# Two weight matrices converted to float32 during the attention, kept in DRAM, and only split later

## The chip, the cores and the metric

The kernel runs on one core of one Trainium2 chip. A core has four computing engines, each with its own instruction queue that runs in order: TensorE (matmul), VectorE, ScalarE and GpSimd. SyncE (SP) issues the DMAs; they too are issued in the order of its queue, so a DMA that waits for a semaphore holds back those behind it. The metric is the time of one execution in microseconds (us). The kernel before takes 804.85 us, the median of 3 runs (803.93 to 806.13).

## The reference, cut

Causal attention with a bias from cumulative sums, then a product of gated projections, then a second feed-forward block with a softmax-weighted activation and a layer norm:

```python
attn_out = attention(q, k, v, s)              # B=4, H=8, S=576, D=64
x = attn_out.transpose(0, 2, 1, 3).reshape(B * S, H * D)      # 2304 x 512
# first block: w1, w2 512x1024, w3 1024x1024, w_out 1024x512
a = x @ w1;  b = x @ w2
x = (a * b @ w3) @ w_out
# second block: w_in 512x1024, w_out2 1024x512, g_ln 1024
h = x @ w_in
solu = h * softmax(h)
ln = (solu - mean(solu)) / sqrt(var(solu) + 1e-6) * g_ln
return ln @ w_out2
```

The six weight matrices arrive as float64. The kernel takes their bit patterns as pairs of 32-bit words and makes float32 of them on the chip.

## The kernel before, in words

**Precision.** TensorE multiplies in a reduced float32 format. Each operand is therefore held as two words, a high one (a copy rounded to that format, `hi`, mostly on ScalarE) and a low one (the rest, `lo`, a subtraction on VectorE or GpSimd), and each product is three matmuls: high by high, high by low, low by high. Names that end in H and L (or h and l) are such pairs.

**Conversion of a weight.** A `stage` tile holds 128 x 512 float64 values (512 KB) as word pairs. `to_f32` (L365) makes float32 of them in place: one scaling of the high words on GpSimd (L371) or ScalarE (L369), then three integer instructions on VectorE (L375, L376, L379). `split_w` (L384) then writes high and low word. `w_job` queues a load and its conversion; `pump(n)` converts n queued tiles and reloads the stage buffers that come free.

**Stages**, with their place in the traced execution:
- Attention, 0 to about 376 us: 32 heads in steps (L504 to 567), scores, softmax, transposes of the probabilities (`tr`), product with v (`av`). The matmuls of a = x w1 and b = x w2 of finished batches (`ab_unit`, L310) are filled in between. During steps 3 to 16, `PUMP` converts the 16 tiles of w1 and w2. g = a b goes to DRAM (`g_scr`).
- The last batch of `ab_unit`, about 376 to 424 us, beside the conversion of w_out (8 tiles) and of the first w3 tiles (16 in all).
- M = w3 w_out, 424 to 468 us: eight blocks `m_unit(f)` (L585) of 24 matmuls into PSUM, each copied out as MH (ScalarE) and ML (VectorE). After each block `pump(AM[f])` converts three more tiles, first the rest of w3, then the eight of w_in (into IH and IL, L744 to 751).
- Second phase, from 468 us: `x2_unit` (x2 = g M in chunks of 256 tokens, L654), `h_unit` (h = x2 w_in and the chain of the layer norm, L678), `tr2` (L714) transposes the normalised tile `so`, `out_unit` (L728) multiplies by w_out2. The eight tiles of w_out2 are converted, scaled by g_ln on ScalarE (L771) and split into OH and OL by `wo2_conv` (L769) during the first x2 and h units.

The order of instructions on each engine is made by a scheduler at build time from the order of the program's text and modelled durations. It decides where a conversion stands in an engine's queue.

Of the kernel before, what the change touches and what calls it, by code (L numbers as in the profile page):

```python
# [25 lines left out]
def tile_attention_moe(  # L26
# [42 lines left out]
    const = ctx.enter_context(tc.tile_pool(name="const", bufs=1, side="left"))  # L69

    g_scr = [dram.tile([KF, 128, S], F32, name=f"g_scr{n}") for n in range(B)]
    cum_scr = dram.tile([NH, 2, S], F32R, name="cum_scr")
# [23 lines left out]
    def lo(dst, src, hi_, eng=nc.vector):  # L96
        eng.tensor_tensor(out=dst, in0=src, in1=hi_.bitcast(F32), op=ALU.subtract)  # L97
# [266 lines left out]

    def to_f32(raw, eng=nc.gpsimd):  # L365

# [3 lines left out]
        else:  # L370
# [6 lines left out]
            out=low, in0=high, scalar=3, in1=low, op0=ALU.logical_shift_left, op1=ALU.bitwise_or,  # L377
        )
        nc.vector.scalar_tensor_tensor(  # L379
            out=low, in0=high, scalar=0x80000000, in1=low, op0=ALU.bitwise_and, op1=ALU.bitwise_or,  # L380
        )
        return low.bitcast(F32)

# [10 lines left out]
    MAT = ()  # L394
    WO2 = (0, 4, 0, 0, 0, 2, 2)
    XMS = ((0,), (1,), (2,), (3,))
    EX = 0
    AP3, AM = (2, 2, 2, 2, 2, 2, 1, 1), (3, 3, 3, 3, 3, 3, 3, 3)
    mjobs = []
# [36 lines left out]
    def wab_job(f, w):  # L436
        fs = slice((f % 4) * 128, (f % 4) * 128 + 128)
        w_job(
            (w1, w2)[w][f],
            lambda: (wab[f // 4][2 * w][:, :, fs], wab[f // 4][2 * w + 1][:, :, fs]),  # L440
            WENG[f] if not isinstance(WENG[f], tuple) else WENG[f][w],
        )


# [48 lines left out]
    for f in range(KF):  # L493
        for w in range(2):
            wab_job(f, w)
    load_jobs()


# [5 lines left out]
    PD, AVO = 10, 2  # L504
    PUMP = {3: 1, 5: 1, 7: 1, 8: 1, 9: 1, 10: 1, 11: 1, 12: 2, 13: 2, 14: 2, 15: 2, 16: 1}
    fill = []
# [64 lines left out]
    ML = pm.tile([128, KF, DM], F32R, name="ML")  # L571
    stg[:] = pm, 4
    mctx = ExitStack()
    mp = mctx.enter_context(tc.tile_pool(name="mp", bufs=1, side="left"))
    WOH = mp.tile([128, KF, DM], F32R, name="WOH")
    WOL = mp.tile([128, KF, DM], F32R, name="WOL")
# [166 lines left out]
    load_g(1)  # L743
    win = []  # L744
    for i in range(8):
        c, o = divmod(i, 2)
        fs = slice(o * 512, o * 512 + 512)
        w_job(
            w_in[c * 128:c * 128 + 128, o * 1024:o * 1024 + 1024],
            lambda c=c, fs=fs: (IH[:, c, fs], IL[:, c, fs]),  # L750
        )
    for f in range(nm[0], KF):
        m_unit(f)
        pump(AM[f] if f < KF - 1 else len(jobs) + len(loaded))
        if f == 4:
            split_g(0, 0)
        if f == 5:
            split_g(0, 1)
# [3 lines left out]
    OL = p2.tile([128, KF, DM], F32R, name="OL")  # L762
    raws = {}

    def wo2_load(k):
        if k < KF:
            raws[k] = stage(wo2[k * 128:k * 128 + 128])

    def wo2_conv(k):  # L769
        t = to_f32(raws.pop(k), G)  # L770
        nc.scalar.activation(out=t, in_=t, func=AF.Copy, scale=gln[:, k:k + 1])  # L771
        hi(OH[:, k], t)
        lo(OL[:, k], t, OH[:, k], nc.gpsimd)
        wo2_load(k + 4)

    nwo = [0]

    def wo2_pump(c):
        for _ in range(c):
            wo2_conv(nwo[0])  # L780
            nwo[0] += 1

    for k in range(4):
        wo2_load(k)
    wo2_pump(WO2[0])
    for i, ms in enumerate(XMS):
        x2_unit(0, *ms)
        wo2_pump(WO2[1 + i])
    split_g(1, 0)
# [5 lines left out]
    for t in range(NT + 2):  # L795
# [9 lines left out]
        if t < 2:  # L805
            wo2_pump(WO2[5 + t])
        if 0 <= t - 2 < NT:
# [57 lines left out]
```

## Time and profile before

| | us |
|---|---|
| median of 3 runs | 804.85 (803.93 to 806.13) |
| profiled execution | 805.43 |
| its span on the core | 803.6 |
| TensorE busy | 764.2 |
| VectorE busy | 454.8 |
| ScalarE busy | 350.9 |
| GpSimd busy | 264.0 |

The span runs from the first to the last instruction. Busy time is the time in which an engine has at least one instruction under way. Matmuls overlap, so a stream of them counts as fully busy even when one starts every 0.12 us and lasts 0.28; the pauses of TensorE are what the table of waits shows. In the rows further down PE is TensorE, PEld its weight loads, DVE VectorE, ACT ScalarE and POOL GpSimd; L12 is line 12 of the kernel; an operation is written out<-in.

### The profile page before, as it was taken

What the parts mean: (1) busy time and instruction counts of PE and PEld (TensorE: products, weight loads), DVE (VectorE), ACT (ScalarE), POOL (GpSimd) and SP (SyncE); (2) the same over time, 40 slices, a digit from 0 to 9 for tenths busy, and PEclk for the clock granted to TensorE, in tenths of its full rate; (3) what the DMA queues carried; (4) which work ended last, traced back from release to release, by engine and by line L of the source; (5) the groups of instructions that cost most, each with busy time, mean ns of one, the idle gap of its engine ahead of it and who ended that gap; (6) DMA issues with size and microseconds to landing.
All of it is one profiled execution on the core that took longest, in us unless ns stands there. A gap on an engine that the chain in (4) does not pass through costs nothing.

```text
span 803.6 us, 13134 instructions
## 1 busy us (share of the span) xinstructions
PE 764.2 (95%) x4848; PEld 652.4 (81%) x4848; DVE 454.8 (57%) x1057; ACT 350.9 (44%) x847; POOL 264.0 (33%) x339
## 2 busy tenths in 40 slices
PE   4897979999999999999999979899999999999997
PEld 2554878888888889888988868788888888888886
DVE  5687688766444554424995999835344243533231
ACT  3674556676545555322434434624333232432231
POOL 7757385967445534201432445400000000000000
PEclk9898999999999999999999989999999999999999
DMA  6344343543333231013668655122020200000001
GB/s 164 109 149 141 113 137 117 148 104 96 99 104 91 76 91 45 31 46 141 209 199 265 226 174 172 58 66 66 14 66 14 67 25 14 14 14 14 14 28 39
DMA packets 38040, 75.59 MB, mean 94 GB/s; under 512 B 6796, under 2 KB 18060, under 8 KB 37976
## 3 DMA queue, kind: packets, MB, share of 16 engines
q1 hardware_dynamic: 37976, 74.76, 30.3%
q8 instruction: 38, 0.62, 0.3%
q14 instruction: 26, 0.21, 0.1%
HBM read 60.36 MB, written 14.38 MB: 93 GB/s over the span
## 4 chain that ended last, share of the span: by engine, by line
PE 79%; DVE 10%; DMA 5%; issue 3%; POOL 2%; ACT 1%; SPq 0%; DVEq 0%; POOLq 0%; ACTq 0%
PE o L734 13%; PE h L685 11%; PE b L333 10%; PE x L665 10%; PE a L333 10%; PE av L305 7%; PE tr L273 4%; PE m L591 3%; PE sc L183 3%; DVE stage L376 3%; DVE stage L375 3%; DMA stage<-in_w_dram 2%; PE sc L191 2%; PE sc L192 2%; PE tr L723 2%
## 5 line engine op out<-in xcount | busy, mean ns | idle before, releaser
L209 ACT ACTIVATE P<-P,STAT 64x64 f32<-64x64 f32 (+4 forms) x160 | 88.2, 553 | 72.3 <-DVE STAT L205 72.0
L241 POOL TENSOR_SCALAR P<-P,STAT 128x576 f32<-128x576 f32 (+4 forms) x160 | 87.0, 563 | 38.7 <-DVE STAT L237 36.5
L707 POOL TENSOR_TENSOR sv<-sv,mhalf 128x1 f32<-128x1 f32 x18 | 10.0, 555 | 262.1 <-DVE sv L704 262.1
L205 DVE CUSTOM_DVE_ANT_0 P<-sc,wmask 64x64 f32<-64x64 f32 (+4 forms) x160 | 71.6, 482 | 26.8 <-PE sc L192 14.5
L693 DVE TENSOR_REDUCE sv<-h 128x1 f32<-128x1024 f32 x18 | 22.0, 1224 | 114.1 <-PE h L685 114.1
L665 PE MATMUL x<-gh,MH 128*128 128x256 f32 x288 | 83.1, 289 | 3.7 <-ACT MH L92 3.7
L665 PE MATMUL x<-gh,ML 128*128 128x256 f32 x288 | 81.5, 284 | 2.1 <-DVE ML L97 2.1
L665 PE MATMUL x<-gl,MH 128*128 128x256 f32 x288 | 81.7, 284 | 0.0
L97 POOL TENSOR_TENSOR QA<-qk,QB 64x576 fp32r<-64x576 f32 x24 | 37.9, 1581 | 84.2 <-ACT QB L92 75.6
L371 POOL TENSOR_SCALAR stage<-stage 128x512 f32<-128x512 f32 x40 | 33.1, 829 | 95.2 <-PE a L333 37.0
L333 PE MATMUL b<-xT0h,W 128*128 128x288 f32 x256 | 60.7, 308 | 3.3 <-DVE g_sb L353 3.2
L94 DVE COPY PT<-tr 64x128 f32<-64x128 f32 (+5 forms) x112 | 41.1, 383 | 34.5 <-ACT PT L92 11.0
L333 PE MATMUL b<-xT1h,W 128*128 128x288 f32 x256 | 59.3, 303 | 1.3 <-ACT a_sb L345 0.7
L333 PE MATMUL a<-xT0h,W 128*128 128x288 f32 x256 | 59.4, 306 | 0.0
L665 PEld LDWEIGHTS x<-gh,MH 128*128 128x128 f32 x288 | 55.5, 193 | 4.7 <-ACT MH L92 3.9
L305 PE MATMUL av<-PT,vr 64*64 64x64 f32 (+4 forms) x384 | 57.9, 414 | 0.3 <-DVE PT L94 0.3
L333 PE MATMUL a<-xT1h,W 128*128 128x288 f32 x256 | 58.0, 300 | 0.0
L353 DVE TENSOR_TENSOR g_sb<-b,a_sb 128x288 f32<-128x288 f32 x64 | 28.7, 452 | 51.3 <-PE b L333 27.7
L734 PE MATMUL o<-OH,lh 128*128 128x512 f32 x144 | 57.2, 397 | 0.3 <-ACT lh L92 0.3
L685 PE MATMUL h<-IH,x2l 128*128 128x512 f32 x144 | 56.7, 394 | 0.8 <-DVE x2l L97 0.8
L665 PEld LDWEIGHTS x<-gh,ML 128*128 128x128 f32 x288 | 55.4, 193 | 2.4 <-DVE ML L97 2.3
L734 PE MATMUL o<-OH,ll 128*128 128x512 f32 x144 | 57.1, 396 | 0.0
(121 smaller groups left out, 2022.8 us busy)
## 6 DMA issues: line engine op xcount, KB each, us to landing
stage<-in_w_dram SPq DMA_DIRECT2D x32, 512.0 KB
qk<-in_qk_dram SPq DMA_DIRECT2D x48, 288.0 KB
g_scr<-g_sb SPq DMA_DIRECT2D x32, 288.0 KB
stage<-in_wo_dram SPq DMA_DIRECT2D x16, 512.0 KB
graw<-g_scr SPq DMA_DIRECT2D x6, 1024.0 KB
out_dram<-o SPq DMA_DIRECT2D x18, 256.0 KB
vr<-in_vm_dram SPq DMA_DIRECT2D x16, 256.0 KB
stage<-in_w_in_dram SPq DMA_DIRECT2D x8, 512.0 KB
```

The source lines that it names most:

```text
L94: eng.tensor_copy(out=dst, in_=src)
L97: eng.tensor_tensor(out=dst, in0=src, in1=hi_.bitcast(F32), op=ALU.subtract)
L205: nc.vector.tensor_tensor_reduce(out=dst2, in0=ps_in, in1=msk, scale=-SCALE, scalar=BIG, op0=ALU.add, op1=ALU.min, accum_out=st[0:rows, ti ...
L209: nc.scalar.activation(out=dst, in_=dst, func=AF.Exp, bias=st[0:rows, ti:ti + 1], scale=-1.0, accum_out=st[0:rows, 5 + ti:6 + ti],)
L241: nc.gpsimd.tensor_scalar(out=dst, in0=dst, scalar1=r, scalar2=1.0, op0=ALU.mult, op1=ALU.mult)
L273: nc.tensor.transpose(ps[:, c:c + 128], pt[:, QOF[i] + 128 * j:QOF[i] + 128 * j + 128], ident)
L305: nc.tensor.matmul(st["ps"][64 * e:64 * e + 64, 448 + c0:448 + c1], vr[0:rows, j, e], PT[(2 * p + e) % 4][0:rows, o + c0:o + c1], **kw,)
L333: nc.tensor.matmul(ps, w_[:, c, fs], x_[:, c, sl], start=(c == 0 and w_ is WH and x_ is XH), stop=(c == KC - 1 and w_ is WL),)
L371: eng.tensor_scalar(out=high.bitcast(F32), in0=high.bitcast(F32), scalar1=2.0 ** -112, scalar2=1.0, op0=ALU.mult, op1=ALU.mult,)
L665: nc.tensor.matmul(ps[m], w_[:, k, m * 128:m * 128 + 128], g_[:, k], start=(k == 0 and w_ is MH and g_ is GH), stop=(k == KF - 1 and w_ is ...
L685: nc.tensor.matmul(ps[:, hf], x_[:, k, ts_], w_[:, k, hf * 512:hf * 512 + 512], start=(k == 0 and x_ is XH and w_ is IH), stop=(k == KC - ...
L734: nc.tensor.matmul(ps, l_[:, k], w_[:, k], start=(k == 0 and l_ is LH and w_ is OH), stop=(k == KF - 1 and l_ is LL),)
```

## The change

The 16 tiles of w_in and w_out2 are no longer converted while M and the second phase run. During steps 19 to 34 of the attention, one a step, each is loaded, converted to float32 (the scaling on ScalarE), w_out2's tiles also scaled by g_ln, written to a new tile `cst` and stored in DRAM (`wf_scr`, 256 KB a tile). While M runs, the float32 tiles are loaded back into four buffers `wf`; `wf_split` makes the high word on ScalarE and the low word on VectorE, one tile of w_in after each `m_unit`, and the eight of w_out2 in the first two rounds of the second phase's loop. `AM` now converts two tiles after each of the first five blocks of M and none after the others. The stage buffers lie in the pool of M's operands instead of the longer-lived one.

```diff
+    wf_scr = [dram.tile([128, CW], F32, name=f"wf_scr{i}") for i in range(16)]
...
-    def to_f32(raw, eng=nc.gpsimd):
+    def to_f32(raw, eng=nc.gpsimd, dst=None):
...
+        res = low if dst is None else dst.bitcast(U32)
         nc.vector.scalar_tensor_tensor(
-            out=low, in0=high, scalar=0x80000000, in1=low, op0=ALU.bitwise_and, op1=ALU.bitwise_or,
+            out=res, in0=high, scalar=0x80000000, in1=low, op0=ALU.bitwise_and, op1=ALU.bitwise_or,
         )
-        return low.bitcast(F32)
+        return res.bitcast(F32)
...
-    WO2 = (0, 4, 0, 0, 0, 2, 2)
...
-    AP3, AM = (2, 2, 2, 2, 2, 2, 1, 1), (3, 3, 3, 3, 3, 3, 3, 3)
+    AP3, AM = (2, 2, 2, 2, 2, 2, 1, 1), (2, 2, 2, 2, 2, 0, 0, 0)
...
+    def spill_job(i):
+        src = w_in[i // 2 * 128:i // 2 * 128 + 128, i % 2 * 1024:i % 2 * 1024 + 1024] if i < 8 else wo2[(i - 8) * 128:(i - 7) * 128]
+
+        def conv(raw):
+            t = at.tile([128, CW], F32, tag="cst", bufs=2, name="cst")
+            to_f32(raw, None, t)
+            if i >= 8:
+                nc.scalar.activation(out=t, in_=t, func=AF.Copy, scale=gln[:, i - 8:i - 7])
+            nc.sync.dma_start(out=wf_scr[i], in_=t)
+
+        jobs.append((src, conv))
...
+    for i in range(16):
+        spill_job(i)
...
-    PUMP = {3: 1, 5: 1, ..., 15: 2, 16: 1}
+    PUMP = {3: 1, 5: 1, ..., 15: 2, 16: 1, 19: 1, 20: 1, ..., 33: 1, 34: 1}
...
-    stg[:] = pm, 4
...
+    stg[:] = mp, 4
...
-    win = []
-    for i in range(8):
-        ...
-        w_job(w_in[...], lambda c=c, fs=fs: (IH[:, c, fs], IL[:, c, fs]))
+    wf = {}
+
+    def wf_load(i):
+        if i < 16:
+            wf[i] = r2.tile([128, CW], F32, tag="wf", bufs=4, name="wf")
+            nc.sync.dma_start(out=wf[i], in_=wf_scr[i])
+
+    def wf_split(i, eng):
+        t = wf.pop(i)
+        if i < 8:
+            c, fs = i // 2, slice(i % 2 * 512, i % 2 * 512 + 512)
+            h_, l_ = IH[:, c, fs], IL[:, c, fs]
+        else:
+            h_, l_ = OH[:, i - 8], OL[:, i - 8]
+        hi(h_, t)
+        lo(l_, t, h_, eng)
+        wf_load(i + 4)
+
+    for i in range(4):
+        wf_load(i)
     for f in range(nm[0], KF):
         m_unit(f)
-        pump(AM[f] if f < KF - 1 else len(jobs) + len(loaded))
+        pump(AM[f])
+        wf_split(f, V)
...
-    def wo2_conv(k):
-        ...
...
         if t < 2:
-            wo2_pump(WO2[5 + t])
+            for k in range(4):
+                wf_split(8 + 4 * t + k, V)
```

What VectorE has in its queue around the last blocks of M and the first units of x2. Before, from the low word of block 5 on (IL is the low word of w_in, stage any tile under conversion):

```order
L97 TENSOR_TENSOR ML<-m,MH 128x512
L379 SCALAR_TENSOR_TENSOR stage<-stage 128x512
L376 SCALAR_TENSOR_TENSOR stage<-stage 128x512
L375 TENSOR_SCALAR stage<-stage 128x512
L379 SCALAR_TENSOR_TENSOR stage<-stage 128x512
L97 TENSOR_TENSOR IL<-stage,IH 128x512
L376 SCALAR_TENSOR_TENSOR stage<-stage 128x512
L375 TENSOR_SCALAR stage<-stage 128x512
L379 SCALAR_TENSOR_TENSOR stage<-stage 128x512
L97 TENSOR_TENSOR ML<-m,MH 128x512
```

The same place on VectorE in the changed kernel, from the last conversion row of w3 on (OL is the low word of w_out2, wf a float32 tile that was loaded back):

```order
L382 SCALAR_TENSOR_TENSOR stage<-stage 128x512
L99 TENSOR_TENSOR w3l<-stage,w3h 128x512
L99 TENSOR_TENSOR ML<-m,MH 128x512 x2
L99 TENSOR_TENSOR OL<-wf,OH 128x512 x4
L99 TENSOR_TENSOR x2l<-x_5346,x2h 128x256
L99 TENSOR_TENSOR x2l<-x_5373,x2h 128x256
L99 TENSOR_TENSOR OL<-wf,OH 128x512 x3
L99 TENSOR_TENSOR x2l<-x_5400,x2h 128x256
L99 TENSOR_TENSOR OL<-wf,OH 128x512
L99 TENSOR_TENSOR x2l<-x_5427,x2h 128x256
L99 TENSOR_TENSOR gl<-graw,gh 128x512 x4
L709 TENSOR_REDUCE sv<-h 128x1
```

The conversion rows of w_in that stood between the ML rows are gone, and so are those of w_out2 between the x2l rows; in their place stand one subtraction a tile, those of w_out2 behind the last ML.

What SP issues while M runs. Before (graw are loads of g, in_w_dram is w3, the others are w_in and w_out2):

```order
L633 DMA graw<-g_scr_66 128x8x256 x2
L414 DMA stage<-in_w_dram 128x1024 x2
L633 DMA graw<-g_scr_66 128x8x64
L633 DMA graw<-g_scr_67 128x8x192
L414 DMA stage<-in_w_dram 128x1024
L633 DMA graw<-g_scr_67 128x8x256
L414 DMA stage<-in_w_dram 128x1024 x4
L414 DMA stage<-in_w_in_dram 128x1024 x8
L414 DMA stage<-in_wo_dram 128x1024 x5
```

SP at the same place in the changed kernel, up to the last w3 load:

```order
L765 DMA wf<-wf_scr_68 128x512
L416 DMA stage<-in_w_dram 128x1024
L765 DMA wf<-wf_scr_69 128x512
L416 DMA stage<-in_w_dram 128x1024
L649 DMA graw<-g_scr_82 128x8x64
L649 DMA graw<-g_scr_83 128x8x192
L416 DMA stage<-in_w_dram 128x1024
L649 DMA graw<-g_scr_83 128x8x256
L765 DMA wf<-wf_scr_70 128x512
L765 DMA wf<-wf_scr_71 128x512
L416 DMA stage<-in_w_dram 128x1024
L765 DMA wf<-wf_scr_72 128x512
```

The loads of float32 tiles stand between those of w3, eight of them (the first two ahead of this piece, one more behind it) ahead of the last three w3 loads; loads of w_in stood behind all w3 loads.

A conversion in the attention of the changed kernel, as VectorE has it in one head's step (L207 is the softmax's first pass, L96 a copy out of PSUM, L355 the product g):

```order
L377 TENSOR_SCALAR stage<-stage 128x512
L378 SCALAR_TENSOR_TENSOR stage<-stage 128x512
L207 ISA P,STAT_116<-sc,wmask 128x320
L207 ISA STAT_116 128x1
L207 ISA P,STAT_116<-sc,wmask 128x192
L207 ISA STAT_116 128x1
L96 CAST QA<-qk_2466 64x576
L382 SCALAR_TENSOR_TENSOR cst<-stage 128x512
L355 TENSOR_TENSOR g_sb<-b,a_sb 128x288
```

Its three instructions stand between those of the softmax; in the kernel before the same rows stand there without them.

## Rows read from the trace of the kernel before

**Rows 1.** The page: busy us, share, instructions; and the chain by engine

```profile
PE 764.2 (95%) x4848; PEld 652.4 (81%) x4848; DVE 454.8 (57%) x1057; ACT 350.9 (44%) x847; POOL 264.0 (33%) x339
...
PE 79%; DVE 10%; DMA 5%; issue 3%; POOL 2%; ACT 1%; SPq 0%; DVEq 0%; POOLq 0%; ACTq 0%
```

**Rows 2.** Busy by stretch: length, each engine's us (instructions), clock, DMA share, GB/s

```profile
80.00:120.00 40.00, 35.44 (x241) 30.96 (x239) 30.84 (x72) 21.10 (x56) 23.84 (x28) 0.96 0.40 121
120.00:160.00 40.00, 39.96 (x300) 34.24 (x298) 32.49 (x84) 25.05 (x72) 29.81 (x32) 1.00 0.45 134
160.00:360.00 200.00, 200.00 (x1499) 173.23 (x1498) 96.94 (x325) 105.08 (x306) 88.00 (x118) 1.00 0.28 78
424.00:468.00 44.00, 43.70 (x193) 36.22 (x194) 35.11 (x52) 18.81 (x32) 15.66 (x12) 1.00 0.73 237
468.00:525.00 57.00, 46.95 (x298) 43.02 (x297) 50.77 (x80) 29.19 (x52) 26.53 (x24) 0.91 0.41 131
525.00:800.00 275.00, 274.62 (x1577) 239.12 (x1575) 104.57 (x210) 87.02 (x163) 8.77 (x16) 1.00 0.10 32
```

**Rows 3.** TensorE's waits, 468 to 525: us, times, longest

```profile
PE x L665 <- ACT MH L92: 3.7, 1, 3.7
PE tr L723 <- DVE so L708: 3.5, 1, 3.5
PE x L665 <- DVE ML L97: 2.1, 1, 2.1
PE h L685 <- DVE x2l L97: 0.8, 1, 0.8
```

**Rows 4.** Timeline of VectorE and ScalarE: start us, duration us, instruction

```profile
471.78 0.68 DVE L97 TENSOR_TENSOR ML<-m,MH 128x512 fp32r<-128x512 f32 x1
...
476.51 0.59 ACT L92 ACTIVATE MH<-m 128x512 fp32r<-128x512 f32 x1
```

**Rows 5.** Busy by stretch, as rows 2, around two pauses

```profile
477.20:481.10 3.90, 3.90 (x18) 3.90 (x19) 3.39 (x5) 1.43 (x3) 2.56 (x3) 0.50 0.45 139
481.40:487.20 5.80, 5.80 (x52) 5.80 (x52) 5.45 (x10) 2.13 (x4) 2.97 (x4) 1.00 0.76 246
512.40:515.30 2.90, 2.90 (x14) 2.90 (x15) 2.19 (x5) 1.82 (x4) 1.07 (x1) 0.50 0.00 0
```

**Rows 6.** Groups by line, 424 to 525: count, busy us, mean ns, idle before

```profile
L376 DVE SCALAR_TENSOR_TENSOR stage<-stage 128x512 uint32<-128x512 uint32 x23 | 20.2, 877 | 0.8 <-POOL stage L371 0.5
L379 DVE SCALAR_TENSOR_TENSOR stage<-stage 128x512 uint32<-128x512 uint32 x23 | 19.0, 825 | 0.1
L375 DVE TENSOR_SCALAR stage<-stage 128x512 uint32<-128x512 uint32 x23 | 16.0, 695 | 1.3 <-DMA stage<-in_wo_dram 0.8 <-DMA stage<-in_w_in_dram 0.3
L371 POOL TENSOR_SCALAR stage<-stage 128x512 f32<-128x512 f32 x16 | 14.9, 931 | 23.9 <-DMA stage<-in_w_dram 7.7 <-DMA stage<-in_wo_dram 4.7 <-DMA stage<-in_w_in_dram 4.0
L97 POOL TENSOR_TENSOR OL<-stage,OH 128x512 fp32r<-128x512 f32 x8 | 12.7, 1603 | 5.7 <-ACT OH L92 5.7
...
L369 ACT ACTIVATE stage<-stage 128x512 f32<-128x512 f32 x7 | 4.7, 674 | 6.1 <-DMA stage<-in_w_in_dram 6.1
```

**Rows 7.** The chain in order of time: start us, us, matmuls

```profile
534.41 5.49 PE h L685 x24
539.90 2.81 PE x L665 x24
```

**Rows 8.** Timeline of GpSimd and VectorE near the last w3 tiles

```profile
453.28 1.90 POOL L97 TENSOR_TENSOR w3l<-stage,w3h 128x512 fp32r<-128x512 f32 x1 [3.23 <-ACT w3h L92]
...
453.93 1.80 DVE L376 SCALAR_TENSOR_TENSOR stage<-stage 128x512 uint32<-128x512 uint32 x1
461.09 1.15 DVE L97 TENSOR_TENSOR w3l<-stage,w3h 128x512 fp32r<-128x512 f32 x1
```

**Rows 9.** Busy by stretch, as rows 2, while M runs

```profile
428.00:448.00 20.00, 20.00 (x90) 16.54 (x90) 15.64 (x23) 9.57 (x17) 7.68 (x5) 1.00 1.04 340
448.00:468.00 20.00, 20.00 (x90) 16.58 (x89) 19.04 (x29) 8.57 (x14) 7.98 (x7) 1.00 0.50 164
```

More of the change, by code (lines that the diff above doesn't have):

```diff
@@ L504, in tile_attention_moe @@
     PD, AVO = 10, 2
-    PUMP = {3: 1, 5: 1, 7: 1, 8: 1, 9: 1, 10: 1, 11: 1, 12: 2, 13: 2, 14: 2, 15: 2, 16: 1}
+    PUMP = {3: 1, 5: 1, 7: 1, 8: 1, 9: 1, 10: 1, 11: 1, 12: 2, 13: 2, 14: 2, 15: 2, 16: 1, 19: 1, 20: 1, 21: 1, 22: 1, 23: 1, 24: 1, 25: 1, 26: 1, 27: 1, 28: 1, 29: 1, 30: 1, 31: 1, 32: 1, 33: 1, 34: 1}
     fill = []
@@ L743, in tile_attention_moe @@
     load_g(1)
-    win = []
-    for i in range(8):
[L746 to L751, printed above, removed]
+    wf = {}
[15 more added lines that the diff above has]
+        wf_load(i)
     for f in range(nm[0], KF):
         m_unit(f)
-        pump(AM[f] if f < KF - 1 else len(jobs) + len(loaded))
+        pump(AM[f])
+        wf_split(f, V)
         if f == 4:
@@ L762, in tile_attention_moe @@
     OL = p2.tile([128, KF, DM], F32R, name="OL")
[L763 to L767, printed above, removed]
-    def wo2_conv(k):
[L770 to L785, printed above, removed]
     for i, ms in enumerate(XMS):
         x2_unit(0, *ms)
-        wo2_pump(WO2[1 + i])
     split_g(1, 0)
```

## The prediction

> **What bounds the kernel now.** I read the page's sums and chain first, then the busy time by stretch, then what TensorE waited for in the one stretch where it stands still late in the run, and only then the rows of VectorE and ScalarE that it waited for. The page shows TensorE busy for 764.2 us of 803.6 and a chain that is 79% TensorE [rows 1]. The stretches show where the rest lies [rows 2]. From 160 to 360 us (the attention) TensorE is busy for all 200 us, and VectorE for 97 and ScalarE for 105 of them. From 424 to 468 (the product M) it is full too. From 525 to 800 (the second phase) it is full again, with VectorE at 105 of 275. Between them, from 468 to 525, VectorE is busy for 50.8 of 57 us, TensorE has only 46.95, and its granted clock is 0.91. So one stretch of 57 us late in the kernel is set by VectorE and the rest by TensorE. That stretch is the one which the change empties.
>
> What TensorE waits for there are four things [rows 3]: the high word of the last M block (3.7 us), the low word of the M block before it (2.1), the normalised row tile of the second phase (3.5) and a low word of x2 (0.8), 10.1 us in all. None of them needs w_in or w_out2. The rows show why they are late [rows 4]: the low word of M block 6 starts on VectorE at 471.78, and its matmuls had ended by about 462.3 (the 424 to 468 row has 193 matmuls in 43.70 us [rows 2], so 226 ns each, 5.43 us a block of 24, and seven blocks from 424.3); MH of block 7 starts on ScalarE at 476.51, 8.5 us after the end of its matmuls at 468. Both engines work in order, and conversions of w_in, some of them waiting for their DMA, stand ahead.
>
> The pauses also cost clock [rows 5]. After the pause that ends at 477.15 TensorE is granted 0.50 (1.2 GHz) and 18 matmuls take 3.90 us; back at 1.00 (2.4 GHz) 52 of the same take 5.80. That is 217 against 112 ns, so 18 x 0.105 = 1.9 us lost. The pause that ends at 512.37 is followed by 2.90 us at 0.50, of which half, 1.45 us, is lost.
>
> **The change part by part, and the sum.** The profiled execution took 805.43 us for a span of 803.6, 0.6 above the median of 804.85; the sum is made against 805.43.
>
> *Removed in the stretch.* Sixteen conversions (eight of w_in, eight of w_out2) leave 424 to 525. Each has three VectorE instructions of 877, 825 and 695 ns there [rows 6], so 16 x 2.40 = 38.4 us of VectorE. On GpSimd twelve scalings of 931 ns go (all of w_out2, half of w_in) and twelve low-word subtractions of about 1.6 us, 30 us in all. On ScalarE eight g_ln scalings and four word scalings go, some 9 us. *Added there.* The twelve subtractions move to VectorE, at 0.68 us each [rows 4], 8.2 us; the high words stay on ScalarE. VectorE's net is minus 30 us of the 86 it has from 424 to 525 [rows 2]. Then it is no longer what ends last. The order shows the same: ahead of the last two ML rows there now stand only w3 conversions, the four OL rows come behind both, and behind the second-phase row maximum no conversion is left. All four waits of [rows 3] have lost what made them late. With the clock that is 10.1 + 1.9 + 1.45 = 13.4 us. As a check from the other side: the stretch holds 216 matmuls of x2 at 2.81/24 us, 72 of h at 5.49/24 [rows 7] (counted in the order) and 8 transposes that I put at 1 us together, 25.3 + 16.5 + 1.0 = 42.8 of 57 us, so 14.2 are lost. I take 14.0 as all there is to win.
>
> *What is late next.* The M product needs its 16 halves of w3, one each the weights of 12 matmuls. In the kernel before the last low half starts on VectorE at 461.09 and takes 1.15 [rows 8]; TensorE reads it from 468 - 12 x 0.226 = 465.3, so the margin is 3.0 us. The change pushes on it from two sides. SP's order puts eight loads of float32 copies (256 KB each, 2.1 MB) in front of the last w3 loads, on a queue that is saturated from 428 to 448: 340 GB/s at a DMA share of 1.04 [rows 9]. If all 2.1 MB fall ahead of the last w3 half at that rate they take 6.2 us. But the queue then falls to 164 GB/s and half share from 448 to 468 [rows 9], and the order pulls two matmuls of the last block and eighteen of x2 in front of the last w3 halves (2 x 0.226 + 18 x 0.117 = 2.6 us of cover). On the other side VectorE loses the w_in conversions there. GpSimd's remaining w3 subtractions still stretch VectorE: 1.80 us for an L376 beside a GpSimd subtraction of 1.90 us, against 877 mean [rows 6, 8]. From below: no wait (6.2 - 3.0 - 2.6 is about nothing, and VectorE is freer); from above: the whole 6.2 us, plus 1.9 for the clock, 8.1. I walked the after order with these durations and found the halves of block 6 just in time; I take 2.0 us, near the lower end, and keep 0 to 8.1.
>
> *Added in the attention.* Sixteen conversions at one a step, sixteen steps that fill about the 200 us from 160 to 360. Each is a ScalarE scaling (674 ns), three VectorE instructions (2.40 us) [rows 6], for the eight of w_out2 a further ScalarE pass that I put at the same, and on SP a 512 KB load and a 256 KB store. That is 38 us of VectorE on 97 and 16 of ScalarE on 105 [rows 2]: 135 and 121 of 200. SP waits in front of each store until VectorE or ScalarE has written it; behind it stand the q and k loads of two heads ahead, the cum rows and the g stores. A step is some 12 us (200/16) and the loads are two ahead, so a store that is late by a few us stays covered. The bounds come from the two stretches that already do this. From 120 to 160 with four to five conversions in 40 us, GpSimd doing part of them, VectorE is at 32.5 and TensorE still at 39.96: cost nothing. From 80 to 120 TensorE has 35.44 of 40 with VectorE at 30.8 [rows 2]: 4.6 us per 40, which over 200 us is 23. The nearer row is 120 to 160 (the same fill matmuls, full clock, a heavier load than is to come), so I take 0.5. Below nothing is excluded, since TensorE is already full and no wait of it is removed there.
>
> *Elsewhere.* Stage buffers that move from one pool to the other, and the 424 us before M: same order, nothing. The splits of w_out2 wait for no DMA on the chain; out_unit reads them, by the order, behind 240 matmuls of x2 and 72 of h, over 40 us.
>
> Sum: 805.4 - 14.0 + 2.0 + 0.5 = 793.9, so 794.
>
> A page speaks against part of this. The Trainium skill, "DMA: Bandwidth & Descriptors", section "Bandwidth", advises batches of 1 MiB and more and gives 341 GB/s there and 138 at 64 KB; the 256 KB pieces fall between, and by an estimate of mine from these two, 240, the 2.1 MB would cost 8.7 us instead of 6.2. By that the sum would be 796 to 797; that page measured single transfers, and no row here shows a saturated stretch of 256 KB pieces.
>
> **The rivals.** (1) *w3 becomes the wait.* The upper bound above, 8.1 us, falls on the chain: 805.4 - 14.0 + 8.1 + 0.5 = 800.0. For it: the saturated queue and a margin of 3.0 us. Against: the half-empty queue behind it. (2) *The attention stops being covered*, and the kernel ends slower: the conversions sit in VectorE's and ScalarE's order ahead of PSUM evictions, the full TensorE of 160 to 360 turns into that of 80 to 120, 23 us: 805.4 - 14 + 2 + 23 = 816. It decides from 14 - 2 = 12 us, that is 2.4 us of standing in each 40. For it: each conversion holds VectorE for over 2 us at a stretch; against: 120 to 160. (3) *The change does not do what it says*: M's evictions on ScalarE stay in order behind high-word splits that wait for the float32 copies' DMA as they did behind w_in, so that the 3.7 and 2.1 and their 1.9 of clock stay, half of rival 1's 8.1 comes on top, and only the second pause goes: 805.4 - 14 + 7.7 + 4 = 803.1. For it: ScalarE in the after order still has four such splits between M's evictions; against: SP's order has eight of these loads ahead of the last w3 loads, and had those of w_in behind them.
>
> **How the numbers follow.** My forecast (790 to 798) 0.65, rival 1 (798 to 802.4) 0.20, rival 3 0.07, rival 2 0.08. A difference under 0.3%, 2.4 us, can't be told from none here. Forecast and rival 1 are faster, 0.85; rival 3 is the same, 0.07; rival 2 slower, 0.08. The range for 8 in 10 goes from 789.5 (nothing new waits, and a little more comes off than the check shows) to 802 (rival 1 with its clock): it leaves out rivals 2 and 3 and a small tail below.
>
> **What would show it.** Right: from 468 to 525 no wait of TensorE for MH, ML or the normalised tile over 1 us, granted clock 1.00 there, VectorE below two thirds; 160 to 360 still full; any new wait on w3 inside the M product under 3 us. The step on w3 is wrong if TensorE waits there for 5 us or more, the step on the attention if 160 to 360 shows 2 us or more of idle time. The whole is wrong if the time is over 802.

## The result and the profile after

The changed kernel takes 810.77 us (median of 6 runs, 808.99 to 815.45), the kernel before 804.39 (6 runs, 802.53 to 806.13). The ratio is 1.0087, 95% interval 1.006 to 1.0113. It is slower by about 0.9%, where 794.0 in a range of 789.5 to 802.0 was forecast. The profiled execution took 813.74 us with a span of 812.0.

The page of the changed kernel, busy time and chain by engine, against [rows 1]:

```profile
PE 764.9 (94%) x4848; PEld 651.2 (80%) x4848; DVE 459.4 (57%) x1069; ACT 355.9 (44%) x859; POOL 240.6 (30%) x315
...
PE 69%; DMA 11%; DVE 8%; ACT 3%; issue 3%; POOL 2%; SPq 2%; ACTq 0%; DVEq 0%; POOLq 0%
```

TensorE has the same work. Its share of the chain fell from 79 to 69%, and DMA's rose from 5 to 11. The busy time by stretch, columns as in [rows 2], shows in which stretch:

```profile
160.00:360.00 200.00, 188.63 (x1373) 161.47 (x1371) 129.03 (x369) 117.10 (x329) 98.24 (x122) 0.98 0.45 134
424.00:468.00 44.00, 42.22 (x238) 37.18 (x236) 33.84 (x57) 20.05 (x37) 13.66 (x10) 1.00 0.76 249
468.00:525.00 57.00, 54.79 (x336) 48.30 (x335) 35.99 (x61) 23.26 (x43) 6.94 (x6) 1.00 0.32 109
525.00:812.00 287.00, 282.92 (x1625) 246.13 (x1623) 108.97 (x217) 90.74 (x171) 9.32 (x17) 1.00 0.10 32
```

The first row is new: TensorE is no longer full from 160 to 360 us. The third is near what was forecast: 54.79 of 57 busy, granted clock 1.00 against 0.91, VectorE at 36.0 against 50.8.

Stretches of two traces don't hold the same work once one runs late (the third row here still has the end of M in it), so I also compared them matmul by matmul: each matmul of a trace is matched with the same one (same operands, same occurrence) of the kernel before, and the difference of the start times is taken, the median over those within 3 us of a mark on the clock of the kernel before. Positive is late, in us:

| mark, us | 140 | 165 | 194 | 292 | 345 | 424 | 798 |
|---|---|---|---|---|---|---|---|
| changed kernel | 1.6 | 5.2 | 5.4 | 15.2 | 20.3 | 19.6 | 8.4 |

Between 140 and 345 us 18.7 us are lost; after that 11.9 come back. The 1.6 at 140 stand ahead of the first spill conversion; other kernels of this study with the same instructions there stood between 2.4 ahead and 2.0 behind, so I read nothing into it.

TensorE's waits of the changed kernel, 140 to 400 us (us, times, longest), are small and many, and none names a spill tile:

```profile
PE tr L279 <- ACT PT L94: 4.7, 4, 2.1
PE sc L193 <- POOL KB L99: 2.3, 2, 1.4
PE a L335 <- ACT a_sb L347: 2.1, 2, 1.1
```

The pauses are 13.2 us of the 18.7 (1.8 of the 20 us from 140 to 160, 11.4 from 160 to 360). A part of the rest is clock. Soon after pauses of 1.9 us (to 273.4) and 2.1 us (to 325.6) TensorE was granted 0.50 (1.2 GHz) for some 3.4 us each, where the kernel before has 1.00 from 160 to 360 [rows 2]. That is some 1.7 us lost each time, an estimate from these clocks:

```profile
274.50:277.70 3.20, 3.20 (x15) 3.01 (x15) 1.58 (x7) 0.87 (x2) 0.00 (x0) 0.50 0.89 304
325.70:328.90 3.20, 3.20 (x14) 2.93 (x15) 2.35 (x11) 1.68 (x5) 2.08 (x5) 0.50 0.53 201
```

What stood behind the waits is in the groups by line of ScalarE and VectorE, 160 to 360 us (count, busy us, mean ns, then idle time just before and what ended it):

```profile
L382 DVE SCALAR_TENSOR_TENSOR cst<-stage 128x512 uint32<-128x512 uint32 x15 | 14.9, 990 | 0.0
...
L371 ACT ACTIVATE stage<-stage 128x512 f32<-128x512 f32 x14 | 9.7, 690 | 30.4 <-DMA stage<-in_wo_dram 20.6 <-DMA stage<-in_w_in_dram 9.7
L377 DVE TENSOR_SCALAR stage<-stage 128x512 uint32<-128x512 uint32 x14 | 9.4, 670 | 38.1 <-DMA stage<-in_wo_dram 26.4 <-DMA stage<-in_w_in_dram 11.7
L453 ACT ACTIVATE cst<-cst,gln 128x512 f32<-128x512 f32 x8 | 5.8, 719 | 8.4 <-DVE cst L382 8.4
```

The first instruction of nearly every conversion finds its raw tile not yet landed. ScalarE stands 30 us for it and VectorE 38, each with the evictions, q copies and softmax of the attention queued behind. One turn of it, from the timelines of SP's queue, ScalarE and GpSimd (start us, duration us; in brackets the idle time before):

```profile
246.00 1.18 SPq L133 DMA_DIRECT2D qk<-in_qk_dram  x2
247.22 0.58 SPq L416 DMA_DIRECT2D stage<-in_wo_dram  x1
...
258.49 0.34 SPq L454 DMA_DIRECT2D wf_scr<-cst  x1
258.94 1.12 SPq L133 DMA_DIRECT2D qk<-in_qk_dram  x2
```

```profile
253.00 0.70 ACT L371 ACTIVATE stage<-stage 128x512 f32<-128x512 f32 x1 [3.15 <-DMA stage<-in_wo_dram]
...
255.00 0.68 ACT L94 ACTIVATE QB<-qk 64x576 fp32r<-64x576 f32 x1
...
257.75 0.71 ACT L453 ACTIVATE cst<-cst,gln 128x512 f32<-128x512 f32 x1
```

```profile
255.82 1.56 POOL L99 TENSOR_TENSOR QA<-qk,QB 64x576 fp32r<-64x576 f32 x1 [6.84 <-ACT QB L94]
257.32 1.44 POOL L99 TENSOR_TENSOR KB<-qk,KA 64x576 fp32r<-64x576 f32 x1
```

The raw load goes out at 247.22 and lands at 253.00 (5.8 us). ScalarE scales it, then copies q at 255.00; GpSimd's two subtractions end at 258.76, and with them the q and k buffer is free. On another way the same tile's last pass on ScalarE (L453) ends at 258.46, and SP, which stood in front of the store of this tile from 251.3 on, issues it at 258.49. The two ways end within 0.3 us of each other. Then SP issues the next q and k load at 258.94, with the next raw load tied behind it. Of the nine q and k loads from 209.48 to 308.29 us, four were released by the subtraction; the other five went out behind a store for which SP had waited 4.3 to 7.3 us, with no further wait for their buffer. Either way this is a closed round, since the q copy and the store both come behind a conversion that waits for the raw load. Its first and last q and k issue here, nine heads apart, and those of the kernel before, eight apart:

```profile
196.25 1.12 SPq L133 DMA_DIRECT2D qk<-in_qk_dram  x2
...
308.29 1.74 SPq L133 DMA_DIRECT2D qk<-in_qk_dram  x2
```

```profile
198.95 1.12 SPq L131 DMA_DIRECT2D qk<-in_qk_dram  x2
...
291.07 1.11 SPq L131 DMA_DIRECT2D qk<-in_qk_dram  x2
```

That is 112.04/9 = 12.45 us a head against 92.12/8 = 11.52.

### The profile page after: what moved, and what is told of

It reads as the page before. It is cut to its first block, busy times and chain, and to the rows that moved or that the text cites. A ratio compares the mean times of both kernels' runs of the same rounds, so it can differ in the third digit from the quotient of the medians.

```text
span 812.0 us, 13194 instructions
## 1 busy us (share of the span) xinstructions
PE 764.9 (94%) x4848; PEld 651.2 (80%) x4848; DVE 459.4 (57%) x1069; ACT 355.9 (44%) x859; POOL 240.6 (30%) x315
## 4 chain that ended last, share of the span: by engine, by line
PE 69%; DMA 11%; DVE 8%; ACT 3%; issue 3%; POOL 2%; SPq 2%; ACTq 0%; DVEq 0%; POOLq 0%
PE o L750 12%; PE x L681 12%; PE h L701 12%; PE b L335 7%; PE a L335 7%; PE av L307 5%; DMA stage<-in_w_dram 4%; PE tr L275 3%; DMA stage<-in_wo_dram 3%; PE sc L185 2%; DVE stage L377 2%; PE tr L739 2%; DVE stage L378 2%; PE sc L193 2%; PE sc L194 2%
## 5 line engine op out<-in xcount | busy, mean ns | idle before, releaser
L243 POOL TENSOR_SCALAR P<-P,STAT 128x576 f32<-128x576 f32 (+4 forms) x160 | 89.0, 575 | 51.2 <-DVE STAT L239 47.3
L207 DVE CUSTOM_DVE_ANT_0 P<-sc,wmask 64x64 f32<-64x64 f32 (+4 forms) x160 | 71.8, 481 | 20.2 <-PE sc L185 11.7
L377 DVE TENSOR_SCALAR stage<-stage 128x512 uint32<-128x512 uint32 x56 | 37.8, 675 | 54.2 <-DMA stage<-in_wo_dram 29.2
L750 PE MATMUL o<-OL,lh 128*128 128x512 f32 x144 | 56.8, 395 | 0.0
L701 PE MATMUL h<-IL,x2h 128*128 128x512 f32 x144 | 56.5, 392 | 0.0
L701 PE MATMUL h<-IH,x2h 128*128 128x512 f32 x144 | 56.2, 390 | 0.0
L681 PEld LDWEIGHTS x<-gl,MH 128*128 128x128 f32 x288 | 54.2, 188 | 0.9
```

Of the source, the lines that this page charges most:

```text
L207: nc.vector.tensor_tensor_reduce(out=dst2, in0=ps_in, in1=msk, scale=-SCALE, scalar=BIG, op0=ALU.add, op1=ALU.min, accum_out=st[0:rows, ti ...
L243: nc.gpsimd.tensor_scalar(out=dst, in0=dst, scalar1=r, scalar2=1.0, op0=ALU.mult, op1=ALU.mult)
L377: nc.vector.tensor_scalar(out=low, in0=low, scalar1=29, scalar2=None, op0=ALU.logical_shift_right)
L681: nc.tensor.matmul(ps[m], w_[:, k, m * 128:m * 128 + 128], g_[:, k], start=(k == 0 and w_ is MH and g_ is GH), stop=(k == KF - 1 and w_ is ...
L701: nc.tensor.matmul(ps[:, hf], x_[:, k, ts_], w_[:, k, hf * 512:hf * 512 + 512], start=(k == 0 and x_ is XH and w_ is IH), stop=(k == KC - ...
L750: nc.tensor.matmul(ps, l_[:, k], w_[:, k], start=(k == 0 and l_ is LH and w_ is OH), stop=(k == KF - 1 and l_ is LL),)
```

## The experiments

Theories for the lost 18.7 us: the **loop**, the closed round just described; the **load** (the conversions are simply too much work for VectorE and ScalarE, the reason that rival 2 of the prediction gave); the **traffic** (12 MB of extra loads and stores delay the q and k loads). Each kernel ran 4 to 10 times on a chip with the kernel before, whose medians there were 804.47 (the first four kernels below), 805.98 (pin, pin_fold, early, stage3), 805.05 (halfload, waitdouble, pin_all) and 804.86 (pin_both).

**nospill**: the second half alone.

```diff
-    for i in range(16):
-        spill_job(i)
...
-            nc.sync.dma_start(out=wf[i], in_=wf_scr[i])
+            p, q = divmod(i, NP)
+            nc.sync.dma_start(out=wf[i], in_=qkT[p, 2 * q:2 * q + 2].rearrange("h d a s -> (h d) (a s)")[:, 0:CW])
```

> The attention without the 16 loads, conversions and stores; the second phase as in the changed kernel, its float32 tiles loaded from an input tensor instead (256 KB each, so the product with w_in and w_out2 is of other numbers). This prices the second half alone. In the traces the changed kernel is 20.3 us behind the kernel before when M starts and 8.4 us behind at the end, so 11.9 us come back after the attention. All theories: 792 to 794 us, and the M product and the second phase as in the changed kernel. If the 11.9 us were only the slack of a late attention (the loads had more time), 797 or more.

794.02 us, ratio 0.9869 (0.9836 to 0.9902). The gain of the second half is real and needs no late attention. (The tiles that it loads back come from an input tensor, so its products with w_in and w_out2 are of other numbers.)

**noload**: work without wait. 14 of the 16 conversions work again on the two tiles that were loaded. All are tied as in *pin* below, and so they stand at the place that they have in *pin*, behind a q copy, and not at that of the changed kernel, as the expectation has it.

```diff
+            if src is None:
+                loaded.append((old[len(old) % 2 + nold[0] % 2], conv))
...
-        jobs.append((src, conv))
+        jobs.append((src if i < 2 else None, conv))
```

> The conversions of the attention are all there, at the place in each step where the changed kernel has them, but only the first two raw tiles are loaded; the other 14 conversions work again on those two tiles (their numbers are wrong then). Loop theory (ScalarE and VectorE stand, in order, in front of a raw tile that is still on its way; the copies of q and k behind them are late, GpSimd after them, then SP's next q and k load, and behind it the next raw load): the wait is gone, 793 to 797 us. Load theory (38 us of VectorE and 16 of ScalarE are simply too much for these 200 us): 807 to 812. Traffic theory (8 MB of loads and 4 MB of stores slow the q and k loads): between, 797 to 803.

794.81 us, ratio 0.9872 (0.9845 to 0.9898). VectorE has 25.7 us more to do than in the kernel before [rows 2], and TensorE is full:

```profile
160.00:360.00 200.00, 200.00 (x1489) 172.68 (x1488) 122.64 (x370) 117.45 (x331) 96.47 (x115) 1.00 0.33 98
```

The load theory falls as far as this place goes: all the work, without the wait, costs nothing there. What the work would cost at the changed kernel's own place without a wait was not tried.

**waitonly**: wait and traffic, almost no work.

```diff
-            t = at.tile([128, CW], F32, tag="cst", bufs=2, name="cst")
-            to_f32(raw, None, t)
-            if i >= 8:
-                nc.scalar.activation(out=t, in_=t, func=AF.Copy, scale=gln[:, i - 8:i - 7])
+            t = csts[i % 2]
+            low, high = raw[:, 0:1, 0], raw[:, 0:1, 1]
+            nc.scalar.activation(out=high.bitcast(F32), in_=high.bitcast(F32), func=AF.Copy, scale=2.0 ** -112)
+            nc.vector.tensor_scalar(out=t.bitcast(U32)[:, 0:1], in0=low, scalar1=29, scalar2=None, op0=ALU.logical_shift_right)
...
```

> All 16 loads and stores of the attention are there, but the conversion works on one column of the tile instead of 512 (one ScalarE and one VectorE instruction, both still waiting for the raw tile; a constant tile is stored). So nearly no work, but the wait and the traffic. Loop theory: most of the loss stays, 804 to 811 us. Load theory: 793 to 796. Traffic theory: 804 to 811.

795.29 us, ratio 0.9885 (0.9864 to 0.9905), TensorE full from 160 to 360. The loop theory missed here as I had written it. ScalarE still waited for landings, for 18.7 us against 33.8 in the changed kernel (140 to 340 us), and q and k loads came 11.6 us apart. So this much waiting, with next to no work behind it, does not do it either; the time is the one that the load theory gave.

**trafficonly**: the loads and stores, and no engine reads the raw tiles.

```diff
-            t = at.tile([128, CW], F32, tag="cst", bufs=2, name="cst")
-            to_f32(raw, None, t)
-            if i >= 8:
-                nc.scalar.activation(out=t, in_=t, func=AF.Copy, scale=gln[:, i - 8:i - 7])
+            t = csts[i % 2]
...
```

> All 16 loads and stores of the attention, and no engine reads the raw tiles: no conversion, no wait of ScalarE or VectorE; a constant tile is stored. Loop theory: 793 to 796 us. Load theory: 793 to 796. Traffic theory: 804 to 811.

796.17 us, ratio 0.9879 (0.9826 to 0.9931). The traffic theory falls.

The work (at another place), a shorter wait and the traffic cost nothing, each by itself; together they cost 18.7 us. What remained was that the conversion stands where its tile has not landed, with its full work on top. The order shows why it stands there. Rows of ScalarE's and SP's order of the changed kernel (number in the order, line, out<-in; `stage_3076` is one raw tile, `qk2_2901` and `qk2_3058` the q and k of two heads in succession):

```text
303 L371 ACTIVATE stage_3076<-stage_3076 128x512
304 L94 ACTIVATE QB0_103<-qk2_2901 64x576

170 L133 DMA qk2_3058<-in_qk_dram 64x1152 x2
171 L416 DMA stage_3076<-in_wo2_dram 128x1024
```

The load stands behind the loads of the later head, 3058, and the conversion ahead of the copies of the earlier one, 2901. The program text has it two steps after its load; the scheduler took it forward, presumably to where the tile is there by its modelled durations.

**pin**: the whole changed kernel, with each conversion tied on both engines behind the first softmax instructions of its own step.

```diff
-        nc.vector.tensor_tensor_reduce(
+        hold2[0] = nc.vector.tensor_tensor_reduce(
...
-        nc.scalar.activation(
+        hold2[1] = nc.scalar.activation(
...
-        pump(PUMP.get(st, 0))
+        if st < 19:
+            pump(PUMP.get(st, 0))
+        else:
+            with tc.issue_after(hold2[0].ins), tc.issue_after(hold2[1].ins):
+                pump(PUMP.get(st, 0))
```

> The whole changed kernel, all loads, conversions and stores; only each conversion is tied, on ScalarE and VectorE, behind the first softmax instructions of its own step. In the order it so comes one step later, two heads behind its load instead of one, and SP's order has its load ahead of the q and k load of the next head. The runs before left the two simple theories without support: work without the wait costs nothing (794.8), wait and traffic without the work cost nothing (795.3, 796.2). Loop theory, sharper: only both together make the round (q and k load issue, raw load landing 5.8 us, ScalarE's scaling and q copy, GpSimd's two subtractions, next issue) longer than the 11.5 us of a step. A load that has a step more time takes the landing out of the round: 793 to 797 us, with the q and k loads 11.5 us apart from 200 to 290 us. Rival (work and traffic together are too much, wherever the conversion stands): 805 to 812.

795.37 us, ratio 0.9865 (0.9841 to 0.9889): 10.6 us under the kernel before, and this one computes the whole reference. The same tile's conversion now stands at row 339 of ScalarE's order, behind the q copy of the head after 3058, and its load at row 177 of SP's. In the trace of pin, the tile of the turn shown above is loaded at 248.51 and its conversion starts at 268.29 us, 19.8 later; in the changed kernel it was 5.8. So two things changed at once: the tile has time to land, and the conversion no longer stands ahead of a q copy that the next loads need.

```profile
248.51 0.41 SPq L417 DMA_DIRECT2D stage<-in_wo_dram  x1
...
268.29 0.66 ACT L372 ACTIVATE stage<-stage 128x512 f32<-128x512 f32 x1
```

Groups of pin, 160 to 360 us (its lines are one higher):

```profile
L383 DVE SCALAR_TENSOR_TENSOR cst<-stage 128x512 uint32<-128x512 uint32 x16 | 12.0, 747 | 0.1
L372 ACT ACTIVATE stage<-stage 128x512 f32<-128x512 f32 x16 | 10.6, 663 | 0.0
L378 DVE TENSOR_SCALAR stage<-stage 128x512 uint32<-128x512 uint32 x16 | 9.9, 620 | 0.0
L454 ACT ACTIVATE cst<-cst,gln 128x512 f32<-128x512 f32 x8 | 5.7, 718 | 6.2 <-DVE cst L383 6.2
```

The same instructions, and not a microsecond of waiting for a load. TensorE waits for nothing from 140 to 400 us, and the stretch is full with as much traffic as in the changed kernel; and as this kernel is not late, the stretch that the change was made for is full too, with VectorE at 29.3 of 57:

```profile
160.00:360.00 200.00, 200.00 (x1489) 172.59 (x1488) 124.74 (x373) 117.61 (x330) 96.39 (x116) 1.00 0.46 135
468.00:525.00 57.00, 57.00 (x368) 51.64 (x367) 29.32 (x56) 23.20 (x45) 1.67 (x3) 1.00 0.20 56
```

**pin_fold**: pin, and g_ln applied in the split of the second phase instead of in the attention.

```diff
-            if i >= 8:
-                nc.scalar.activation(out=t, in_=t, func=AF.Copy, scale=gln[:, i - 8:i - 7])
...
+            nc.scalar.activation(out=h_, in_=t, func=AF.Copy, scale=g)
+            eng.scalar_tensor_tensor(out=l_, in0=t, scalar=g, in1=h_.bitcast(F32), op0=ALU.mult, op1=ALU.subtract)
```

> As pin, and the scaling of w_out2's tiles by g_ln is taken out of the attention (eight ScalarE passes that wait for VectorE's third conversion instruction) and done inside the split of the second phase: the high word is a scaled copy on ScalarE, the low word one VectorE instruction that scales and subtracts. Loop theory: the round was already short enough, so no more than 1 us against pin: 792 to 797 us. Rival (ScalarE's standing behind VectorE is a part of the loss, 8.4 us of waits in the trace): 2 us or more better than pin.

795.15 us, ratio 0.9864 (0.9844 to 0.9883): no difference from pin. ScalarE's standing behind VectorE (6.2 us in pin) is covered.

**early** and **stage3**: other ways to bring the tile sooner.

```diff
-        if after[0] is None:
+        if after[0] is None or free[0]:
...
+        free[0] = st >= 16
```

> The changed kernel with one line other: the raw loads of the 16 tiles are not tied behind the q and k loads. In the order SP issues them as soon as a buffer is free, and the scheduler puts the conversions right behind them, some 1.5 a step, so that they are done some 80 us sooner. Loop theory: the q and k load no longer stands between one raw load and the next, but the round is now raw load, conversion, buffer free, and ScalarE still stands for each landing: a part comes back, 796 to 804 us. Rival (any conversion that waits for its load costs its wait): as the changed kernel or worse, 808 to 814.

```diff
-    stg = [at, 2]
+    stg = [at, 3]
```

> The changed kernel with three raw buffers instead of two in the attention, nothing else. In the order each load still stands behind a q and k load and each conversion still ahead of the q copy that the next q and k load waits for: the third buffer is spent on converting one step sooner. Loop theory: the round is the same, 808 to 812 us. Rival (the loads wait for a free raw buffer): 793 to 799.

early: 807.13 us, ratio 1.0017 (0.9993 to 1.0042). It missed its own forecast by 3 us. 13 us are lost between 140 and 292 and none after, when all tiles are done; ScalarE waits 12.6 us for landings, and SP 12 for stores, against 55 in the changed kernel (140 to 345 us): so a loss of 13 us comes without long waits for the stores. What the rest is was not separated. stage3: 809.2 us, ratio 1.0041 (1.002 to 1.0063), as the loop theory said. The scheduler spends the third buffer on converting a step sooner, and ScalarE again stands 29.1 us for landings. A sooner load does not help as long as the conversion moves forward with it.

**halfload** and **waitdouble**: the round's length, changed from either side. halfload is the changed kernel with half the bytes in 14 of the raw loads; waitdouble is waitonly with a second 512 KB load ahead of 15 of the raw loads, so it has nearly 8 MB more traffic too.

```diff
+            if 18 < stg[2] <= 32:
+                raw = old.pop(0)
+                with tc.issue_after(after[0].ins):
+                    nc.sync.dma_start(out=flat(raw)[:, 0:CW], in_=src[:, 0:CW])
```

> The changed kernel with the conversions where they stand in it, one head behind their load and ahead of the q copy, all their work and their stores; but from the third tile on only half of a tile is loaded (256 KB, into the same buffer; the other half keeps old numbers). Only the landing gets shorter. Loop theory: by the rows of the changed kernel a round is 12.45 us, of which the landing is 5.8; a landing of some 4 us makes it about 10.7, under the 11.5 of a step, so nearly all comes back: 794 to 800 us. Rival (each conversion costs its wait and its work, whether the round closes or not): the waits of some 3.2 us fall to 1.5, half of the loss comes back, 801 to 806.

```diff
+        if dbl[0]:
+            spare = at.tile([128, CW, 2], U32, tag="spare", bufs=1, name="spare")
+            with tc.issue_after(after[0].ins):
+                nc.sync.dma_start(out=flat(spare), in_=src)
```

> The kernel that waited for its loads but converted one column only (795.3 us), with a second load of 512 KB ahead of each of the raw loads, into a tile that nobody reads. Nearly no work, a longer landing. Loop theory: the round was about 11.3 us there and gets 2 to 3.5 longer; 14 rounds are 2 to 3.3 us over the step of 11.5, 28 to 45 us at most, and some of it covered: 812 to 840 us, with the q and k loads 13 us or more apart. Rival (work is what costs, the wait only adds to it): 794 to 799.

halfload: 804.85 us, ratio 1.0005 (0.9987 to 1.0023). It misses the loop theory's 794 to 800 and lies in its rival's 801 to 806, by which each conversion costs its wait and its work whether the round closes or not. The landing was 4.3 to 5.5 us instead of the 4 that I had put, and the lost time between 140 and 345 is 9.9 instead of 18.7. Its first and last q and k load, nine heads apart:

```profile
196.90 1.34 SPq L133 DMA_DIRECT2D qk<-in_qk_dram  x2
...
301.37 1.47 SPq L133 DMA_DIRECT2D qk<-in_qk_dram  x2
```

That is 11.6 us a head, hardly over the step of 11.52 and 0.8 us in nine heads, and yet 4.3 us were lost between 194 and 292. So the round is not all of the loss. The rival's reason does not fit either: the waits did not halve, ScalarE stood 43.4 us for landings (140 to 340 us) against 33.8 in the changed kernel.

waitdouble: 803.01 us, ratio 0.9977 (0.9946 to 1.0008). It lies between the two forecasts and misses both. The loop theory's direction holds: with almost no work, a longer landing brings a loss back, 7.7 us over waitonly, though the added traffic was not priced apart. SP's queue shows two heads:

```profile
237.89 1.11 SPq L133 DMA_DIRECT2D qk<-in_qk_dram  x2
239.68 0.42 SPq L421 DMA_DIRECT2D stage<-in_wo_dram  x1
...
250.37 1.11 SPq L133 DMA_DIRECT2D qk<-in_qk_dram  x2
```

From 201.25 to 300.21 us there are eight rounds of 12.4, 0.9 over the step; together they are 6.8 us over it, most of the loss.

**pin_all** and **pin_both**: the conversions of w1 and w2 tied too, in all steps (an edit of pin) or up to step 10 (an edit of pin_fold).

```diff
-        if st < 19:
+        if hold2[0] is None:
```

> As pin, with the 16 conversions of w1 and w2 in steps 3 to 16 tied to their own step as well. Loop theory: there too a conversion may stand ahead of its landing, but the waits for a load are only 5 us on VectorE from 0 to 125 us in the trace of pin, so little is to be had: 791 to 796 us. Rival (the idle time of TensorE before 125 us comes from the loads of w1 and w2): below 788.

```diff
-        if st < 19:
+        if 10 < st < 19:
```

> pin_fold, with the conversions of w1 and w2 in steps 3 to 10 tied to their own step too, those of steps 11 to 18 free. Matmul by matmul the trace of pin_all is 10 us ahead of the kernel before at 110 us and only 4.6 at 165, that of pin 0.6 and 1.0: the ties of the early steps win and those of the two-a-step conversions lose. If the early gain is carried through to the end: 785 to 791 us. Rival (the free conversions of steps 11 to 18 lose it again, as 140 to 165 does in pin_all): 793 to 797.

796.04 us, ratio 0.989 (0.9834 to 0.9946), and 792.88 us, ratio 0.9841 (0.9809 to 0.9874), the lowest median of the study. Neither can be told from pin (the intervals overlap). pin_both lies 0.1 us under its rival's 793 to 797 and 1.9 over the 785 to 791 of the other, so that the early gain is carried through is not shown.

The lateness at the marks, worked out as above, for the attention (140 to 345 us) and for what follows (345 to 798):

| kernel | lost, 140 to 345 | back, 345 to 798 |
|---|---|---|
| changed kernel | 18.7 | 11.9 |
| nospill | 0.1 | 9.3 |
| noload | 1.2 | 12.8 |
| waitonly | 0.8 | 9.3 |
| trafficonly | -0.2 | 7.9 |
| pin | 1.4 | 10.6 |
| pin_fold | 0.3 | 10.6 |
| early | 13.0 | 11.6 |
| stage3 | 13.8 | 9.9 |
| halfload | 9.9 | 9.6 |
| waitdouble | 8.5 | 8.4 |

## Why the prediction was wrong

**Removed in the stretch (14.0) and what is late next (2.0): right.** The four waits of [rows 3] are gone, the clock is 1.00. What waits instead are the w3 halves in M; these are all waits there and behind it that are new (424 to 812 us):

```profile
PE m L607 <- ACT w3h L94: 1.8, 2, 1.4
...
PE m L607 <- POOL w3l L99: 0.4, 1, 0.4
```

2.2 us for a term put at 2.0. That it fits so well is in part luck: 2.0 was a choice within 0 to 8.1, made for late loads, and what the w3 halves waited for directly was VectorE's conversion (ScalarE stood 2.48 and 1.44 us for it before the last two high halves that TensorE waited for); how much of that goes back to the loads was not separated. Net 12.0 were forecast after the attention; the traces show 11.9, and nospill by time 10.4 (804.47 - 794.02). Rival 1 (6 us more of w3) and rival 3 did not come. The Trainium skill's caution about pieces under 1 MiB ("DMA: Bandwidth & Descriptors", section "Bandwidth") did not show here. From 448 to 468 us, with pieces of 256 KB among larger ones in the queue, the DMA engines moved 347 GB/s at a share of 1.07; no run has a stretch of such pieces alone.

```profile
448.00:468.00 20.00, 20.00 (x90) 16.53 (x89) 15.21 (x26) 12.35 (x22) 8.74 (x5) 1.00 1.07 347
```

**Added in the attention (0.5): wrong, 18.7.** The step that failed is the sentence that the loads are two ahead, so that a store that is late by a few us stays covered. It was read from the program's text. The order of the changed kernel puts each conversion less than one head behind its load. The prediction counted the work (38 us of VectorE; noload and pin show that it is free at their place) and SP's waits for the stores, but not the wait of ScalarE and VectorE for the raw tile, though [rows 6] had such waits before L369 and L371. With a landing of 5.8 us and 2.4 us of VectorE behind it, every step was pressed, and through GpSimd's subtractions or the store, and SP's q and k loads, it came back to the next raw load. So the stores did count: SP stood up to 7.3 us in front of one, and the q and k loads behind it went out late.

The bound was wide enough (23 us), and the value was taken from the wrong end of it: the row 120 to 160 has four to five conversions whose place in the order, against their landing, I did not look at. Rival 2, at a chance of 0.08, had the place in the order and nearly the size (23 us). What it gave as the reason, over 2 us of VectorE's work a conversion, is not enough: pin has all of that work and loses nothing. It did not have the wait for the tile.

By size: 805.43 + 1.6 (late already at 140 us) + 18.7 - 11.9 = 813.8, the profiled execution's 813.74. The median is 3 us lower, 810.77, so the 18.7 belongs to that execution.

**How far the cause is settled.** Shown: the traffic alone, a shorter wait with next to no work, and the work at pin's place cost nothing; more distance between load and conversion, which also puts it behind the q copies, takes away all of the loss with everything else left in, and with it all waits for a raw tile. Shown by the rows: the closed round of 12.45 us, which gives 112.04 - 9 x 11.52 = 8.4 of the 9.8 us lost from 194 to 292 us. Argued: that the wait, and not the work at that place, makes the round too long. ScalarE stands 2.7 us for the tile in a round on the mean (1.2 to 3.8 from 204 to 303 us); without it the round would be some 9.8 us, an estimate from these rows, and under the step. waitdouble, with next to no work, speaks for it; halfload speaks against the round as the only way, since it lost 4.3 us there at 11.6 us a head. Not tried apart: the 3.6 us at the first tiles (140 to 165) and the 5.1 at the end (292 to 345), where the last two tiles are loaded together at 310 us and converted in one step.

## What to carry to other kernels

When work is moved into a stretch that looks half empty, count for each engine not only its busy time there but what its new first instruction waits for, and read from the order how much lies between a load and the instruction that needs it. The text's distance means nothing if a scheduler moves the consumer forward to a modelled landing; tie the consumer to its own step. And if the load is itself queued behind something that waits for that consumer's engine, the round is a bound of its own: add it up, along each way that leads back (here a buffer and a store), and hold it against the step.

## What was not expected of the hardware

Half the bytes did not halve the landing: 512 KB behind two q and k loads in SP's queue took 5.3 to 6.1 us from issue to the first instruction that waited for it (changed kernel, 210 to 280 us), 256 KB 4.3 to 5.5 (halfload, same stretch). And VectorE's last conversion instruction, of the same shape, took 990 ns on the mean in the changed kernel and 747 in pin. The five of the changed kernel's 15 that lay beside GpSimd's subtractions for 0.98 us or more took 1.31 to 1.79 us, the other ten 0.67 to 1.01. In pin none lay beside them for more than 0.67 us, and none took over 1.01. That the two engines hinder each other was not tried apart.
